# Which queue issues the first transposing loads: x tiles 1 to 3 from ScalarE, the plain loads from SyncE

## The chip, the core and the metric

The kernel runs on one core of a Trainium2 chip. The core has five engines that run side by side, each with an instruction stream of its own: TensorE (PE in the profile, with PEld for its weight loads), VectorE (DVE), ScalarE (ACT), GpSimd (POOL) and SyncE (SP). Data moves between the chip's main memory and the core's on-chip memory by DMA. In this kernel SyncE and ScalarE issue DMAs; the profile shows their issuing as SPq and ACTq, and the two queues that the issued transfers go into as q1 (SyncE's) and q10 (ScalarE's). Sixteen DMA engines serve both.

The metric is device time in microseconds (us) of one execution, median over several runs.

## The reference

One input `x` of 2048 rows by 640 columns goes through a linear-attention block (32 heads of 20) and through a gated feed-forward block (1728 wide), and a sigmoid gate per row mixes the two:

```python
def _A_ref(x, wqkv, wo):
    q, k, v = ...                                  # x @ wqkv, split by head
    phi = lambda t: jnp.where(t > 0, t + 1, jnp.exp(t)) + 1e-6
    pq, pk = phi(q), phi(k)
    kv = jnp.einsum("bhsd,bhse->bhde", pk, v)
    z = jnp.einsum("bhsd->bhd", pk)
    num = jnp.einsum("bhqd,bhde->bhqe", pq, kv)
    den = jnp.einsum("bhqd,bhd->bhq", pq, z)[..., None] + 1e-6
    ...                                            # (num / den) @ wo
def _B_ref(x, w_gate, w_up, w_down):
    return (_gelu(x @ w_gate) * (x @ w_up)) @ w_down

g = _sigmoid((x * gate_w).sum(-1, keepdims=True))
return g * _A_ref(...) + (1 - g) * _B_ref(...)
```

All inputs are bfloat16. Only `x @ wqkv` for the k and q parts, and the gate, matter for the change.

## The kernel before

The kernel is one long program without loops on the chip. A small planner (`_Plan`) takes every operation in program order with the engine it runs on, what it reads and what it writes, and puts in the semaphore waits. Each engine runs its own operations in the order in which they were written down; a DMA counts as an operation of the engine that issues it, and its completion has a semaphore of its own. So there are two kinds of order: the order on each issuing engine, fixed in the text, and the waits between engines, fixed by the data.

The stages are these. First, for each of the 16 row tiles of x (128 rows each), TensorE multiplies the transposed tile `xT` by the k weights `wk` and the q weights `wq` (640 columns each, in 5 slices of 128 rows). ScalarE takes the exponential of each product from PSUM, and VectorE makes `phi` of it. Then come the sums over all rows (`MM`), the feed-forward products (`G`, line 700, the largest part), and the output products (line 864). From tile 4 on the first stage is done by `KQ` (line 539), k and q together. The first four tiles (`NQ = 4`) are done apart: first k for tiles 0 to 3 by `KM` (lines 453 and 454), then q for them by `QM` (lines 468 and 469), so that the work can begin with only the k weights there.

The start, up to the first `QM`, is what the change touches:

- Tile 0 is loaded plainly by `load_x(0)` and transposed on TensorE by `T` (lines 433 and 437). Tiles 1 to 15 come by `load_xT` (line 353), a DMA that transposes on its way. `load_wk(k)` and `load_wq(k)` (through `dma_in`, line 341) load slice k of the weights, 160 KB in 128 rows of 1280 bytes. The gate's weights are a tiny load into `gw_sb`, after VectorE has zeroed it.
- On SyncE the order is x tile 0, wk0, xT1, wk3, wk4, xT2, xT3, wq0 to wq4, xT4 to xT15, and then the large loads. On ScalarE it is the small load `touch`, wk1, wk2, one dummy `Exp` activation, which brings in ScalarE's table, and the gate's weights.
- TensorE runs a few dummy products (`warm`), `T`, and then `KM(n, ks)` for tile n and slices ks: tile 0 with slices 0, 1, 2; tile 1 with slices 0, 1, 2; slice 3 for both tiles; `gate_col` (line 498, which turns the gate's weights into a column of `wq`); slice 4 for both tiles; then tile 2 and tile 3 whole; then `QM`.
- A product of tile n goes into the PSUM banks 2n and 2n+1 (modulo 8), and `gate_col` and `T` use banks 7 and 6 on the way. `phi1` (ScalarE, line 478) and `phi2` (VectorE, lines 488 and 492) empty the banks.

The lines that fix the order on the two issuing engines:

```python
load_x(0); load_wk(0); load_xT(1); load_wk(3); load_wk(4)   # SyncE
load_wk(1, "act"); load_wk(2, "act")                        # ScalarE, after touch
P.op("act", lambda e: e.activation(eg[:, 0:1], zero, ACT.Exp), writes=[r_eg[0]])
dma_in(gw_sb[0:5, :], ..., [r_gw], eng="act")
for i in range(2, NQ): load_xT(i)                           # SyncE again
for k in range(KC): load_wq(k)
for i in range(NQ, NT): load_xT(i)
```

Of the kernel before, what the change touches and what calls it, by code (L numbers as in the profile page):

```python
# [6 lines left out]
ACT = mybir.ActivationFunctionType  # L7
ALU = mybir.AluOpType
BF16 = mybir.dt.bfloat16
F32 = mybir.dt.float32  # L10
# [5 lines left out]
NT = S // 128  # L16
KC = D // 128
# [7 lines left out]
NQ = 4  # L25
# [137 lines left out]
def bass_gated_mix__linear_attn_block__geglu_ffn__prompt_kernel(  # L163
# [63 lines left out]
    with (  # L227
# [8 lines left out]
        with contextlib.ExitStack() as stack:  # L236
            dma_sems = [stack.enter_context(nc.semaphore("s_in%d" % i)) for i in range(n_dma_in)]

            P = _Plan(["pe", "act", "dve", "pool", "sp"])
# [9 lines left out]
            def new_dma_key():  # L249
                k = "in%d" % dma_next[0]  # L250
                dma_next[0] += 1
                return k

            def v16(o, n):
                return pool[:, o:o + n]

            def v32(o, n):
                return pool[:, o:o + 2 * n].bitcast(F32)
# [7 lines left out]
            xT = v16(R_XT, KC * S).rearrange("p (k s) -> p k s", k=KC)  # L266
# [30 lines left out]
            eg = v32(O_EG, 16)  # L297
# [3 lines left out]
            gw_sb = v16(O_GW, 128)  # L301
# [6 lines left out]
            r_xT = [P.sb("xT%d" % i, R_XT, R_XT + KC * S) for i in range(NT)]  # L308
# [25 lines left out]
            r_eg = [P.res("eg%d" % i) for i in range(NT)]  # L334
# [3 lines left out]
            r_gw = P.res("gw")  # L338

            def dma_in(dst, src, writes, reads=(), eng="sp"):  # L340
                P.op(eng, lambda e, dst=dst, src=src: e.dma_start(dst, src),  # L341
                     reads=reads, writes=writes, dma=new_dma_key())
# [3 lines left out]
            def load_x(i, eng="sp"):  # L346
                dma_in(x_aug[:, i, 0:640], A_x[0, i * 128:(i + 1) * 128, :], [r_xn[i]], eng=eng)

            def load_wk(k, eng="sp", after=()):
                dma_in(wk[:, k, :], A_wqkv[k * 128:(k + 1) * 128, 640:1280], [r_wk[k]], reads=after, eng=eng)  # L350

            def load_xT(i, after=()):
                P.op("sp", lambda e: e.dma_start_transpose(xT[:, :, i * 128:(i + 1) * 128],  # L353
                                                           A_x[0, i * 128:(i + 1) * 128, :]),
                     reads=list(after), writes=[r_xT[i]], dma=new_dma_key())

            def load_wq(k, eng="sp"):
                dma_in(wq[:, k, 0:640], A_wqkv[k * 128:(k + 1) * 128, 0:640], [r_wq[k]], eng=eng)


            P.op("act", lambda e: e.dma_start(touch[0:16, 0:4], A_wqkv[0:128:8, 640:644]),
                 writes=[P.res("touch")], dma=new_dma_key())
            load_x(0)
            load_wk(0)
            load_xT(1)
            load_wk(3)
            load_wk(4)
            load_wk(1, "act")
            load_wk(2, "act")

            zero = nc.const_aps.tensor(0.0, (128, 1), F32)
            P.op("act", lambda e: e.activation(eg[:, 0:1], zero, ACT.Exp), writes=[r_eg[0]])
            P.op("dve", lambda e: e.memset(gw_sb, 0.0), writes=[r_gw])
            dma_in(gw_sb[0:5, :], gate_w.rearrange("(k p) -> k p", p=128), [r_gw], eng="act")
            for i in range(2, NQ):
                load_xT(i)
            for k in range(KC):
                load_wq(k)
            for i in range(NQ, NT):
                load_xT(i)  # L380
            dma_in(x_aug[:, NXN:8, 0:640],
                   A_x[0, NXN * 128:8 * 128, :].rearrange("(i p) w -> p i w", p=128), r_xn[NXN:8])
# [32 lines left out]
            def warm(count, n):  # L415
                def fn(e):
                    last = None
                    for w in range(count):
                        last = e.matmul(ps[:, 4, 0:n], one_l, one_r[:, 0:n], start=True, stop=True)
                    return last  # L420
                P.op("pe", fn, writes=[bank[4]])
# [4 lines left out]
            def slot(n):  # L426
                return SLOTS[n % 4]
# [17 lines left out]
            def KM(n, ks):  # L445
                i = seq[n][1]
                b0, b1 = slot(n)

                def fn(e):
                    last = None  # L450
                    for k in ks:
                        lhs = xT[:, k, i * 128:(i + 1) * 128]
                        e.matmul(ps[:, b0, :], lhs, wk[:, k, 0:512], start=(k == 0), stop=(k == KC - 1))  # L453
                        last = e.matmul(ps[:, b1, 0:128], lhs, wk[:, k, 512:640],
                                        start=(k == 0), stop=(k == KC - 1))
                    return last
                P.op("pe", fn, reads=[r_xTa[i] if i < NXN and ks == [0] else r_xT[i]] + [r_wk[k] for k in ks],
                     writes=[bank[b0], bank[b1]])
# [37 lines left out]
            def gate_col():  # L496

                P.op("pe", lambda e: e.matmul(ps[:, 7, 0:5], gw_sb, ident[:, 0:5], start=True, stop=True),
                     reads=[r_gw, r_ident], writes=[bank[7]])
                P.op("dve", lambda e: e.tensor_copy(wq[:, :, 640:641], ps[:, 7, 0:5].unsqueeze(2)),  # L500
                     reads=[bank[7]], writes=[r_gcol])
# [4 lines left out]
            T(0, [0], 7)  # L506
            T(0, [1, 2, 3, 4], 6)
            warm(2, 128)
            for k in range(3):
                KM(0, [k])  # L510
            for k in range(3):
                KM(1, [k])
            KM(0, [3])
            KM(1, [3])
            gate_col()
            KM(0, [4])
            KM(1, [4])
            ALLK = list(range(KC))
            for n in range(2 * NQ):
                if n in (2, 3):  # L520
# [408 lines left out]
```

## Time and profile before

| what | value |
|---|---|
| time, median of 3 runs | 273.87 us (273.7 to 273.97) |
| span of the profiled execution, first to last instruction | 272.6 us |
| median of the runs less that span | 1.27 us |
| TensorE busy | 267.6 us of the span (98%) |
| mean granted TensorE clock | 1.000 |
| DVE / ACT / POOL busy | 140.8 / 75.9 / 30.0 us |
| DMA queue q1 / q10 | 23.22 MB / 0.33 MB |
| TensorE's first `KM` product, first `QM`, first `KQ` | at 4.45, 10.85 and 16.30 us |

A row of the timeline reads: start in us, duration in us, engine, line, operation, what is written and read, and in brackets how long the engine had been idle and what ended it. A row of the chain of waits reads: start, duration, engine or transfer, line. A DMA issue has two times: how long its issuing engine was busy with it, and the time from the start of issue to the landing of the last byte, the completion semaphore included. The stretches that bear on the start are the first 16 us; the table of queues can be asked for any stretch and gives the packets, the bytes and the share of the 16 DMA engines' time.

Issue and landing of each load of the start, in us (issue from the timeline, landing from the time that the list of DMA issues gives for each):

| load | queue | issue starts | landing after | lands at |
|---|---|---|---|---|
| x tile 0 | q1 | 0.79 | 2.2 | 3.0 |
| wk1 | q10 | 1.24 | 3.3 | 4.5 |
| wk0 | q1 | 1.26 | 3.1 | 4.4 |
| xT1 | q1 | 1.71 | 3.8 | 5.5 |
| wk3 | q1 | 3.06 | 3.3 | 6.4 |
| xT2 | q1 | 4.14 | 3.9 | 8.0 |
| wq0 | q1 | 6.72 | 2.7 | 9.4 |
| xT4 | q1 | 9.24 | 4.2 | 13.4 |

### The profile page before, as it was taken

The page shows a single profiled execution, that of the slowest core. Times are in us where ns is not written, and L with a number is a line of the kernel's source. Part 1 is how long each engine was busy: PE and PEld are TensorE (multiplying, and loading weights), DVE is VectorE, ACT ScalarE, POOL GpSimd, SP SyncE. Part 2 cuts the span into 40 slices and gives each one's busy share as a digit, 9 for nine tenths or more (in the row PEclk, how much of TensorE's full clock was granted, in tenths as well). Part 3 has the DMA queues.
Part 4 walks back from the last instruction along what each step waited for, and adds up shares of the span by engine and source line. Part 5 has one row for each costly group of instructions (what it writes and reads, how often), then busy time and mean ns, then how long its engine had stood idle before and what let it go on. Part 6 is the DMA issues. An engine that isn't in the chain of part 4 may idle for free.

```text
span 272.6 us, 3416 instructions
## 1 busy us (share of the span) xinstructions
PE 267.6 (98%) x1341; PEld 127.9 (47%) x1367; DVE 140.8 (52%) x247; ACT 75.9 (28%) x132; POOL 30.0 (11%) x28
## 2 busy tenths in 40 slices
PE   8999999999999999999999999999999999999997
PEld 3555555544445454444444444444444444444444
DVE  1678989997233335999999999634210000000200
ACT  2455555210422453232222233224011122121021
POOL 5000000003240002242332422000000000000000
DMA  7976999600200011514121221273031110110211
GB/s 192 202 115 127 346 399 388 140 2 19 58 19 2 23 50 51 192 34 49 26 48 25 49 48 27 60 219 105 5 77 38 41 38 19 38 41 19 58 58 41
DMA packets 42864, 23.78 MB, mean 87 GB/s; under 512 B 32223, under 2 KB 41439, under 8 KB 42719
## 3 DMA queue, kind: packets, MB, share of 16 engines
q1 hardware_dynamic: 42517, 23.22, 31.9%
q10 hardware_dynamic: 330, 0.33, 0.3%
q8 instruction: 11, 0.18, 0.3%
q14 instruction: 6, 0.05, 0.1%
HBM read 13.83 MB, written 2.63 MB: 60 GB/s over the span
## 4 chain that ended last, share of the span: by engine, by line
PE 96%; DMA 1%; SPq 1%; issue 1%; DVE 0%
PE ps L700 41%; PE ps L864 23%; PE ps L539 12%; PE ps L596 6%; PE ps L843 4%; PE ps L468 2%; PE ps L811 2%; PE ps L678 2%; PE ps L599 1%; DMA pool<-in_A_x_dram 1%; PE ps L453 1%; PE ps L824 1%; SPq L341 1%; PE ps L721 1%; SPq L353 0%
## 5 line engine op out<-in xcount | busy, mean ns | idle before, releaser
L700 PE MATMUL ps<-pool 128*128 128x512 bf16 x510 | 113.0, 379 | 0.5
L700 PEld LDWEIGHTS ps<-pool 128*128 128x128 bf16 x520 | 50.5, 98 | 60.0
L864 PE MATMUL ps<-pool 128*128 128x512 bf16 (+2 forms) x300 | 62.4, 366 | 0.3
L706 ACT ACTIVATE pool<-ps 128x512 f32<-128x512 f32 x52 | 31.0, 597 | 73.1 <-PE ps L700 73.1
L708 DVE TENSOR_TENSOR pool<-ps,pool 128x512 bf16<-128x512 f32 x52 | 34.7, 689 | 31.7 <-PE ps L700 30.4
L864 PEld LDWEIGHTS ps<-pool 128*128 128x128 bf16 x306 | 29.2, 98 | 33.4 <-issue 0.4
L847 DVE TENSOR_TENSOR pool<-ps,pool 128x512 bf16<-128x512 f32 x4 | 2.8, 690 | 61.5 <-PE ps L843 61.5
L539 PE MATMUL ps<-pool 128*128 128x512 bf16 (+1 forms) x176 | 32.5, 343 | 0.2
L754 POOL TENSOR_TENSOR pool<-pool 128x640 f32<-128x640 bf16 x16 | 22.4, 1404 | 73.0 <-DVE pool L756 65.6
L871 ACT ACTIVATE pool<-ps,pool 128x512 bf16<-128x512 f32 (+1 forms) x16 | 10.9, 680 | 68.6 <-PE ps L864 68.6
L539 PEld LDWEIGHTS ps<-pool 128*128 128x128 bf16 x180 | 17.6, 98 | 15.0
L558 DVE SCALAR_TENSOR_TENSOR pool<-ps,pool 128x128 bf16<-128x128 f32 (+2 forms) x36 | 21.7, 602 | 2.1
L549 ACT ACTIVATE pool<-ps 128x640 bf16<-128x640 f32 x24 | 16.9, 703 | 15.8 <-DVE pool L558 9.3
L596 PE MATMUL ps<-pool 128*128 128x512 bf16 x76 | 19.2, 379 | 0.1
L764 DVE TENSOR_TENSOR pool<-pool 128x640 bf16<-128x640 bf16 x16 | 13.2, 826 | 0.6
L762 DVE TENSOR_SCALAR pool<-pool 128x32 f32<-128x32 f32 x16 | 12.8, 802 | 0.6
L756 DVE TENSOR_REDUCE pool<-pool 128x32 f32<-128x640 f32 x16 | 12.9, 808 | 0.0
L644 DVE TENSOR_TENSOR pool<-pool 128x640 f32<-128x640 f32 x14 | 11.6, 826 | 0.5
L843 PE MATMUL ps<-pool 128*128 128x512 bf16 x51 | 11.5, 379 | 0.1
L646 POOL PARTITION_ALL_REDUCE pool<-pool x1 | 4.0, 3971 | 61.0 <-DVE pool L644 61.0
L596 PEld LDWEIGHTS ps<-pool 128*128 128x128 bf16 x78 | 7.0, 98 | 7.3
L555 DVE TENSOR_SCALAR pool<-pool 128x640 bf16<-128x640 bf16 x24 | 7.9, 327 | 1.7 <-ACT pool L549 0.4
(70 smaller groups left out, 124.1 us busy)
## 6 DMA issues: line engine op xcount, KB each, us to landing
out_dram<-pool SPq DMA_DIRECT2D x19, 128.0 KB, 1.7
pool<-in_B_w_gate_dram SPq DMA_DIRECT2D x1, 2080.0 KB, 14.8
pool<-in_B_w_up_dram SPq DMA_DIRECT2D x1, 2080.0 KB, 18.0
pool<-in_A_wqkv_dram SPq DMA_DIRECT2D x8, 160.0 KB, 3.1
pool<-in_A_x_dram SPq DMA_DIRECT2D x1, 1280.0 KB, 9.2
pool<-in_A_x_dram SPq DMA_DIRECT2D x1, 1120.0 KB, 6.3
pool<-in_B_w_down_dram SPq DMA_DIRECT2D x1, 1120.0 KB, 6.4
pool<-omg_row SPq DMA_DIRECT2D x1, 1024.0 KB, 4.8
```

Source lines behind the costliest of these rows:

```text
L539: last = e.matmul(ps[:, b + p, 0:c1 - c0], xT[:, k, i * 128:(i + 1) * 128], wkq[:, k, c0:c1], start=(k == 0), stop=(k == KC - 1))
L549: P.op("act", lambda e: e.activation(e_buf[m], ps_flat[:, o:o + 640], ACT.Exp), reads=banks, writes=[r_e[m]])
L558: P.op("dve", lambda e, c0=c0, c1=c1: e.scalar_tensor_tensor(dst[:, c0:c1], ps_flat[:, o + c0:o + c1], 1.0 + EPS, e_buf[m][:, c0:c1], ALU. ...
L596: last = e.matmul(ps[:, b, :], pk[i][:, c * 128:(c + 1) * 128], x_aug[:, i, 0:512], start=(i == 0), stop=(i == NT - 1))
L700: last = e.matmul(ps[:, b, :], w[:, k, fc * 128:(fc + 1) * 128], xT[:, k, j * 512:(j + 1) * 512], start=(k == 0), stop=(k == KC - 1))
L706: P.op("act", lambda e: e.activation(ge[n], ps[:, gb, :], ACT.Gelu_apprx_tanh), reads=[bank[gb]], writes=[r_ge[n]])
L708: P.op("dve", lambda e: e.tensor_tensor(hT[fc][:, j * 512:(j + 1) * 512], ps[:, ub, :], ge[n], ALU.mult), reads=[bank[ub], r_ge[n]], write ...
L754: P.op("pool", lambda e: e.tensor_tensor(tmp[n], pq[i], z_b, ALU.mult), reads=[r_pq[i], r_zb], writes=[r_tmp[n]])
L756: P.op("dve", lambda e: e.tensor_reduce(den[n], tmp[n].rearrange("p (h d) -> p h d", h=32), AX.X, ALU.add), reads=[r_tmp[n]], writes=[r_de ...
L764: P.op("dve", lambda e: e.tensor_tensor(pq[i].rearrange("p (h d) -> p h d", h=32), pq[i].rearrange("p (h d) -> p h d", h=32), den[n].unsqu ...
L843: last = e.matmul(ps[:, b, :], wd[:, fc, 512:640], hT[fc][:, j * 512:(j + 1) * 512], start=False, stop=(fc == NFC - 2), skip_group_check=True)
L864: last = e.matmul(ps[:, pb, 0:c1 - c0], lhs, rhs, start=False, stop=(q == len(rows) - 1), skip_group_check=True)
```

## The change

The three transposing loads xT1, xT2 and xT3 are issued by ScalarE, after the dummy activation and `touch`; wk1, wk2 and the gate's weights move from ScalarE to SyncE. SyncE's order becomes x tile 0, wk0 to wk4, the gate's weights, wq0 to wq4, xT4 and so on. xT4 is made to wait until xT1, xT2 and xT3 have landed. On TensorE `gate_col` moves from between slice 3 and slice 4 to behind slice 4; the rest of the order stays.

```diff
-            def load_xT(i, after=()):
-                P.op("sp", lambda e: e.dma_start_transpose(xT[:, :, i * 128:(i + 1) * 128],
+            def load_xT(i, after=(), eng="sp"):
+                P.op(eng, lambda e: e.dma_start_transpose(xT[:, :, i * 128:(i + 1) * 128],
                                                            A_x[0, i * 128:(i + 1) * 128, :]),
                      reads=list(after), writes=[r_xT[i]], dma=new_dma_key())
...
+            zero = nc.const_aps.tensor(0.0, (128, 1), F32)
+            P.op("act", lambda e: e.activation(eg[:, 0:1], zero, ACT.Exp), writes=[r_eg[0]])
             P.op("act", lambda e: e.dma_start(touch[0:16, 0:4], A_wqkv[0:128:8, 640:644]),
                  writes=[P.res("touch")], dma=new_dma_key())
             load_x(0)
-            load_wk(0)
-            load_xT(1)
-            load_wk(3)
-            load_wk(4)
-            load_wk(1, "act")
-            load_wk(2, "act")
-
-            zero = nc.const_aps.tensor(0.0, (128, 1), F32)
-            P.op("act", lambda e: e.activation(eg[:, 0:1], zero, ACT.Exp), writes=[r_eg[0]])
+            for i in range(1, NQ):
+                load_xT(i, eng="act")
+            for k in range(KC):
+                load_wk(k)
+
             P.op("dve", lambda e: e.memset(gw_sb, 0.0), writes=[r_gw])
-            dma_in(gw_sb[0:5, :], gate_w.rearrange("(k p) -> k p", p=128), [r_gw], eng="act")
-            for i in range(2, NQ):
-                load_xT(i)
+            dma_in(gw_sb[0:5, :], gate_w.rearrange("(k p) -> k p", p=128), [r_gw])
             for k in range(KC):
                 load_wq(k)
-            for i in range(NQ, NT):
+            load_xT(NQ, after=r_xT[1:NQ])
+            for i in range(NQ + 1, NT):
                 load_xT(i)
...
             warm(2, 128)
-            for k in range(3):
+            for i in range(2):
+                for k in range(3):
+                    KM(i, [k])
+            for k in (3, 4):
                 KM(0, [k])
-            for k in range(3):
                 KM(1, [k])
-            KM(0, [3])
-            KM(1, [3])
             gate_col()
-            KM(0, [4])
-            KM(1, [4])
```

## The prediction

> **What bounds the kernel now.** I read the page first, the parts for busy time and for the chain that ended last. In the chain's lines each engine or line stands with its share of the span.
>
> ```profile
> PE 267.6 (98%) x1341; PEld 127.9 (47%) x1367; DVE 140.8 (52%) x247; ACT 75.9 (28%) x132; POOL 30.0 (11%) x28
> ...
> PE 96%; DMA 1%; SPq 1%; issue 1%; DVE 0%
> ```
>
> TensorE is the bound from the first products to the end. Between 16.3 and 50 us it is busy 33.49 of 33.70 us, and VectorE, the next, 29.97. So whatever moves the first `QM` moves the end by the same amount. What is left besides TensorE lies at the start, and there the chain of waits, in order of time, was read next.
>
> ```profile
> 1.26 0.41 SPq L341
> 1.71 1.30 SPq L353
> 3.06 0.57 SPq L341
> 3.67 0.43 SPq L341
> 4.14 3.93 DMA pool<-in_A_x_dram
> 8.12 0.39 PE ps L453
> ```
>
> The chain is SyncE issuing x tile 0, wk0, xT1 (1.30 us of issue), wk3, wk4, then the landing of xT2, then tile 2's first product. Third, TensorE's timeline there:
>
> ```profile
> 4.45 0.58 PE L453 MATMUL ps<-pool 128*128 128x512 bf16 x1 [0.48 <-DMA pool<-in_A_wqkv_dram]
> ...
> 5.34 0.38 PE L453 MATMUL ps<-pool 128*128 128x512 bf16 x1
> ...
> 7.27 0.38 PE L453 MATMUL ps<-pool 128*128 128x512 bf16 x1
> ...
> 8.12 0.39 PE L453 MATMUL ps<-pool 128*128 128x512 bf16 x1 [0.42 <-DMA pool<-in_A_x_dram]
> ```
>
> A pair (512 and 128 columns) takes 0.27 us from start to start. Twenty pairs are 5.45 us; from 4.45 to 10.85 there are 6.40. The missing 0.95 is 0.35 for the first two pairs, which run slowly (0.89 instead of 0.54), 0.03 for `gate_col`, and 0.58 of waiting for xT2 (8.12 instead of 7.54). Fourth, the table of DMA queues in three stretches (packets, MB, share of 16 engines): 3.2 to 3.6, 4.4 to 4.8, and 6.4 to 7.2 us.
>
> ```profile
> q10 hardware_dynamic: 64, 0.08, 57.7%
> q1 hardware_dynamic: 61, 0.07, 46.9%
> ```
> ```profile
> q1 hardware_dynamic: 410, 0.10, 126.2%
> ```
> ```profile
> q1 hardware_dynamic: 546, 0.13, 82.4%
> ```
>
> In the first, both queues hold rows of weights and take turns, one for one. In the second there is nearly only xT1: packets of 256 bytes, so 640 for a tile's 160 KB, 0.62 us a tile at that rate. In the third xT2 and xT3: 0.94 us a tile. For plain rows, 3.6 to 4.0 had 135 packets in all, so 128 rows take 0.38 us.
>
> **The change, part by part.** Nothing is computed less, and the same bytes move. What can change is when the loads land.
>
> *Issue.* Taken off SyncE ahead of the last wq: three transposing issues, 1.30 + 2.53 = 3.83 us; put on it: wk1, wk2 (0.44 and 0.46 on ScalarE) and the gate's weights (0.57). ScalarE issues `touch` (0.42), then xT1 from about 1.3, xT2 from 2.6, xT3 from 3.9 to 5.2, against 1.71, 4.14 and 5.40 before. SyncE issues wk1 from 1.7 (was 1.24), wk2 from 2.2 (was 1.71), wk3 from 2.6 (was 3.06), wk4 from 3.1 (was 3.67), the gate from 3.5, wq0 to wq4 from 4.1 to 6.6 (was 6.72 to 9.2). What is issued behind them on ScalarE is first `phi1(0)`, at 7.47 before; its queue is free at 5.2, cover 2.2.
>
> *The table load first on ScalarE.*
>
> ```profile
> 2.20 1.28 ACT L372 ACT_TABLE_LOAD   x1 [2.20 <-issue]
> 2.27 0.57 ACTq L341 DMA_DIRECT2D pool<-in_gate_w_dram  x1
> ```
>
> The DMA written behind the activation was issued while the table was still loading. I take 0; the upper bound, if issues had to wait for the activation's end, is 1.28 + 0.20 = 1.48 us on each transposing load.
>
> *Who is served.* This decides. Before, the transposes stood in one queue with wk3 and wk4 and came in turn. Now q10 holds transposes alone and q1 an unbroken row of ten plain loads. No row shows transposes and plain rows contending in two queues for long; 4.0 to 4.4 us, the only stretch with both, has 101 packets on q10 and 126 on q1, but most of the 16 engines had but one of the two. So it is bounded from both sides. (a) Turns by packet, as at 3.2 to 3.6: a 256-byte packet waits for a 1280-byte row each time. Both queues are taken as full from 3.2 (41 packets moved from 2.8 to 3.2, 125 in the 0.4 us after), with half of wk0 still to go: q1 had moved 210 packets from 1.6 to 3.2, 128 of them x tile 0, some 18 small. A plain load then takes 0.38 + 128 of the small packets (0.62 / 640 each, 0.12) = 0.50. wk0 is through at 3.45, wk1 3.95, wk2 4.45, wk3 4.95, wk4 5.45, wq4 7.95; 0.5 more to landing, as xT1's last packets before (about 5.0) stand to its landing at 5.5. xT1 needs 640 turns, 2.5 us: through at 5.7, landed 6.2 (was 5.5). xT2: 576 of its packets by 7.95, the rest at once, landed 8.55 (was 8.04). xT3: 9.2 (was 8.8). TensorE: tile 1 begins at 6.2 and its slices 0 to 2, then slices 3 and 4 of both tiles, are seven pairs, 1.91; wk3 and wk4 have landed by then and stand queued behind tile 1. `gate_col` to 8.14; tile 2 at 8.55; ten pairs, 2.72: first `QM` at 11.27, +0.42. With 0.94 us a transpose instead of 0.62 the same steps give 0.57 a plain load, xT1 at 6.55, xT2 at 9.2, `QM` at 11.92: +1.07. (b) Turns by time, each queue half: a plain load 0.76, a transpose 1.24. wk0 lands at 4.1, wk1 4.85, wk2 5.6, xT1 4.95, wk3 6.35, wk4 7.1, xT2 6.2, xT3 7.4. Tile 0's slice 2 waits until 5.6; from there it and the seven pairs run through with `gate_col` to 7.81, and ten pairs to 10.53: -0.32. I take (a) with the faster transpose, since the only stretch with two full queues shows turns by packet, and xT1's rate was the one with its packets already queued. Rounded up towards the slower row: +0.5.
>
> [...]
>
> *xT4 waits for xT1 to xT3.* The wait on SyncE ends at xT3's landing, about 9.2, against an issue at 9.24 before; behind it stand xT5 to xT15 and all the large loads. xT4 landed 4.2 after its issue, 13.4, and `KQ(4)` began at 16.30: cover 2.9 us. Each `KQ` takes 2.7 us and each further transpose 1.36, so if xT4 isn't late none is. Cost 0; without the cover 1 us per us.
>
> *wq and the gate.* wq0 to wq4 come sooner than they did, and were needed at 10.85 and later: 0. The gate's load was issued at 2.27 and is now at 3.5, behind wk4. Were it as slow as the slowest plain load (3.3), it lands at 6.8; `gate_col` now runs after 8.1: cover 1.3. `gate_col`'s copy (0.18 on VectorE) must be through before tile 3 uses bank 7, five pairs or 1.36 us later. It costs the same 0.03 in its new place.
>
> *Sum.* Against the profiled execution's span of 272.6 us, +0.5 makes 273.1; around the span lie 1.27 us to the median of 273.87, which the change doesn't touch. The forecast is 274.4 us.
>
> **The rivals.** *Served by time*, case (b): 273.87 - 0.32 = 273.55. For it: 4.0 to 4.4 has more small packets than rows. Against it: 64 to 61 in the stretch before. *The transposes run ahead.* If q10's packets are few and start early, nothing waits: with `KM` still at 4.45, 0.58 comes back; if wk0, freed from wk1 beside it, also lands so that tile 0 starts at 4.1, 0.93. Middle 0.75: 273.1, faster. For it: xT2's issue starts 1.5 us sooner, and the wait is the chain's only transfer. Against it: wk1 and wk2 are issued 0.46 later, and five wq loads enter q1 while xT2 and xT3 are under way. This is the case on the other side; it decides once xT1 is landed by 5.4 and xT2 by 7.4. *ScalarE starts late.* The 1.48 us above: xT1 issued at 2.8, lands at 6.6 with its old 3.8; xT2 under case (a) at about 9.6; ten pairs from there give 12.3, +1.45: 275.3. The gate's issue at 2.27 speaks against it. *The change doesn't do what it says* has a form too: if both issuing engines share what makes the packets, the transposes' 1.3 us of issue also hold up the plain loads, the order is as serial as before, and the time lies near 273.9; wk1, on an empty q10, had only 5 packets on that queue before 3.2 though issued at 1.24. It falls between the first two cases and has its chance in (b).
>
> **How the numbers follow.** Forecast, case (a): 0.45; its own range is +0.3 to +1.1, 274.2 to 275.0. Served by time, with the serial form: 0.25. Transposes ahead: 0.18. ScalarE late: 0.12. A difference within 0.2% (0.55 us, so 273.32 to 274.42) is about what a measurement can't tell from no change. Case (a) puts 0.27 above that and 0.18 within; by time 0.21 within, 0.04 faster; ahead 0.16 faster, 0.02 within; late 0.12 slower. Sums: faster 0.20, same 0.41, slower 0.39. The forecast lies at the edge between the two. The range leaves out the best of the cases ahead and the far end of the late one: 273.2 to 275.2.
>
> **What would show it.** In the changed kernel's TensorE timeline, a wait for `in_A_x_dram` ahead of tile 1 (near 5.4 to 6.2) that wasn't there, and tile 2's first product at about 8.5; wk3 landed long before its product. Case (b) shows instead short waits for `in_A_wqkv_dram` in tile 0. The case ahead shows tile 2 right behind `gate_col`, before 7.8. The late case shows the first transposing ACTq issue at 2 us or later. If xT4's landing came after 16, or `phi1(0)` waited for ScalarE's issuing, the parts costed at nothing would be wrong.

## The result, and the profile after

| | before | after |
|---|---|---|
| median | 273.98 us (273.7 to 275.07, 6 runs) | 276.99 us (275.78 to 278.47, 6 runs) |
| ratio, 95% interval | | 1.0108 (1.0085 to 1.013) |
| span of the profiled execution | 272.6 us | 275.6 us |
| first `KM`, first `QM`, first `KQ` | 4.45, 10.85, 16.30 | 4.29, 13.78, 19.23 |

The change costs 3.0 us, about 1.1%; the forecast was 274.4 us, with a range to 275.2. All of it is in the first stretch: from the first `QM` to the end of the span it is 261.78 us before and 261.79 after. The first `QM` is 2.93 us later. The page of the changed kernel, busy time and chain:

```profile
PE 269.7 (98%) x1341; PEld 128.4 (47%) x1367; DVE 140.7 (51%) x247; ACT 76.0 (28%) x132; POOL 30.0 (11%) x28
...
PE 96%; DMA 2%; issue 1%; SPq 0%; DVE 0%
```

TensorE's busy time has grown by 2.1 us with the same 1341 instructions: something runs slower, not only later. The chain of waits at the start:

```profile
1.26 0.41 SPq L341
1.72 0.43 SPq L341
2.19 5.06 DMA pool<-in_A_wqkv_dram
7.29 0.61 PE ps L450
...
8.00 0.43 PE ps L450
...
8.54 0.43 PE ps L450
```

Before, it ran through xT2. Now it runs through wk2, a plain load of 160 KB that takes 5.06 us from its issue at 2.19 to its landing at 7.25, and then through products that follow each other at twice the old distance. TensorE's timeline shows both (lines 450 and 451 are the old 453 and 454):

```profile
4.29 0.59 PE L450 MATMUL ps<-pool 128*128 128x512 bf16 x1
4.67 0.31 PE L451 MATMUL ps<-pool 128*128 128x128 bf16 x1
6.46 0.58 PE L450 MATMUL ps<-pool 128*128 128x512 bf16 x1 [1.48 <-DMA pool<-in_A_wqkv_dram]
...
7.80 0.63 PE L450 MATMUL ps<-pool 128*128 128x512 bf16 x1
...
8.33 0.63 PE L450 MATMUL ps<-pool 128*128 128x512 bf16 x1
...
10.46 0.41 PE L450 MATMUL ps<-pool 128*128 128x512 bf16 x1
...
10.76 0.38 PE L450 MATMUL ps<-pool 128*128 128x512 bf16 x1
```

A wait for wk1 of 1.48 us, and pairs at 0.53 us until 10.46, where they fall to 0.27. Before, that step came at 5.3. The table of queues for 3.2 to 8.2 us (packets, MB, share of the 16 DMA engines), first the kernel before, then the changed one:

```profile
q1 hardware_dynamic: 2416, 0.95, 89.0%
q10 hardware_dynamic: 293, 0.32, 18.2%
```
```profile
q1 hardware_dynamic: 484, 0.56, 71.5%
q10 hardware_dynamic: 1287, 0.32, 44.3%
```

The shares sum to more than 1 in both (107% and 116%): the DMA engines are not short of work. Yet they deliver 0.88 MB instead of 1.27 in these 5 us.

### The profile page after: what moved, and what is told of

Its sections match the earlier page's. It is cut to its first block, busy times and chain, and to the rows that moved or that the text cites. A ratio compares the mean times of both kernels' runs of the same rounds, so it can differ in the third digit from the quotient of the medians.

```text
span 275.6 us, 3417 instructions
## 1 busy us (share of the span) xinstructions
PE 269.7 (98%) x1341; PEld 128.4 (47%) x1367; DVE 140.7 (51%) x247; ACT 76.0 (28%) x132; POOL 30.0 (11%) x28
## 4 chain that ended last, share of the span: by engine, by line
PE 96%; DMA 2%; issue 1%; SPq 0%; DVE 0%
PE ps L695 41%; PE ps L859 23%; PE ps L534 12%; PE ps L591 6%; PE ps L838 4%; PE ps L450 2%; DMA pool<-in_A_wqkv_dram 2%; PE ps L806 2%; PE ps L465 2%; PE ps L673 2%; PE ps L594 1%; PE ps L819 1%; PE ps L451 1%; PE ps L716 1%; SPq L341 0%
## 5 line engine op out<-in xcount | busy, mean ns | idle before, releaser
L695 PE MATMUL ps<-pool 128*128 128x512 bf16 x510 | 113.0, 379 | 0.5
L591 PE MATMUL ps<-pool 128*128 128x512 bf16 x76 | 19.2, 379 | 0.1
L751 DVE TENSOR_REDUCE pool<-pool 128x32 f32<-128x640 f32 x16 | 12.9, 809 | 0.0
L838 PE MATMUL ps<-pool 128*128 128x512 bf16 x51 | 11.5, 379 | 0.1
L450 PE MATMUL ps<-pool 128*128 128x512 bf16 x19 | 7.6, 481 | 1.6 <-DMA pool<-in_A_wqkv_dram 1.5
```

Of the source, the lines that this page charges most:

```text
L591: last = e.matmul(ps[:, b, :], pk[i][:, c * 128:(c + 1) * 128], x_aug[:, i, 0:512], start=(i == 0), stop=(i == NT - 1))
L695: last = e.matmul(ps[:, b, :], w[:, k, fc * 128:(fc + 1) * 128], xT[:, k, j * 512:(j + 1) * 512], start=(k == 0), stop=(k == KC - 1))
L838: last = e.matmul(ps[:, b, :], wd[:, fc, 512:640], hT[fc][:, j * 512:(j + 1) * 512], start=False, stop=(fc == NFC - 2), skip_group_check=True)
```

## The experiments

Theory A: transposing packets in one queue and plain rows in the other hinder each other on the DMA engines, so that the loads land late. Its rivals are named in the expectations. Each expectation was written before its run. Landings are those of each run's profiled execution, issue plus time to landing.

**Plain loads in place of the transposing ones**, in the same 256-byte pieces:

```diff
-                load_xT(i, eng="act")
+                dma_in(xT[:, :, i * 128:(i + 1) * 128],
+                       A_x[0, i * 128:(i + 1) * 128, :].rearrange("p (k s) -> p k s", k=KC), [r_xT[i]], eng="act")
```

> The changed kernel, with x tiles 1 to 3 loaded plainly by ScalarE into the same place, in the same 640 pieces of 256 bytes a tile: the transposition of these three tiles is left out, queues and order stay. Theory A (transposing packets in one queue and plain rows in the other hinder each other on the DMA engines): wk1 lands by about 5.0 us instead of 6.3, wk3 by 7 instead of 9.2, no wait over 0.5 us inside tiles 0 and 1, time 273.0 to 274.0. Rival B (turns by packet between two full queues, whatever is in them): the landings stay within 0.5 us of the changed kernel's and the time is 276 or more.

Measured: 276.22 us, ratio 1.0079 (1.0063 to 1.0095); wk1 at 5.82, wk3 at 7.91, a wait of 1.17 us for wk1. Neither theory's numbers. The queues for 3.2 to 8.2 us:

```profile
q1 hardware_dynamic: 819, 0.93, 54.9%
q10 hardware_dynamic: 1926, 0.48, 42.8%
```

1.41 MB, with as many packets a tile as the transposing loads have (640). So pieces of 256 bytes don't bring what the engines deliver down to 0.88 MB; transposing does. By these rows (share times 16 engines times 5 us, over the packets) a packet on q1 takes 54 ns on average; by the rows of the changed kernel above it takes 118. But 1926 of the small pieces moved on q10 to 819 packets on q1, and wk1 still lands 1.2 us after TensorE wanted it (4.6), and the time is hardly better than after. That was the first sign that the loads are not all of it: pairs stayed at 0.53 us until 9.99.

**The queues swapped**, transposing loads on SyncE, wk0 to wk4 on ScalarE:

```diff
             for i in range(1, NQ):
-                load_xT(i, eng="act")
+                load_xT(i)
             for k in range(KC):
-                load_wk(k)
+                load_wk(k, "act")
```

> The changed kernel with the two queues swapped: SyncE issues xT1 to xT3 behind x tile 0, ScalarE issues wk0 to wk4; the rest of SyncE's order stays. Theory A: the same hindrance, wk3 lands after 8 us, time 275.5 to 277.5. Rival D (a transposing load issued by ScalarE is what is slow): wk3 lands by 6.5, time at most 274.3.

Measured: 277.94 us, 1.0139 (1.0113 to 1.0166), 0.4 above A's range; wk3 at 9.63. With the transposing loads on SyncE the plain rows land as late (wk3 at 9.23 in the changed kernel). D falls.

**Dummy products in the wait for wk1:**

```diff
                     KM(i, [k])
+                    if (i, k) == (0, 0):
+                        warm(3, 512)
```

> The changed kernel with three more dummy products of 512 columns behind the first pair of tile 0, where TensorE waits for wk1 anyway. If the slow pairs (0.53 us each instead of 0.27, eight of them) are the loss (rival C), the first QM comes 2.1 us sooner and the time is 274.9. Under theory A the pairs run at 0.27, but slice 3 can't begin before wk3 lands at 9.2; from there 14 pairs and gate_col are 3.8 us, the first QM is at 13.1 instead of 13.8, time 276.3.

Measured: 276.09 us, 1.0079 (1.0055 to 1.0103), 0.9 below the changed kernel; the first `QM` at 13.05, wk3 at 8.94, wk4 at 9.64. As A has it: from wk4's landing twelve pairs and `gate_col` are 3.3 us, which makes 12.9. With the pairs at 0.27 from 8.26 on, what remains is the late landing.

**wq0 to wq4 held back** until xT1 and xT2 have landed (`load_wq` hands `after` on as reads):

```diff
-                load_wq(k)
+                load_wq(k, after=r_xT[1:3])
```

> The changed kernel with wq0 held on SyncE, and all behind it, until xT1 and xT2 have landed, so that only wk0 to wk4 and the gate's weights stand in q1 beside the transposing loads. Rival B in the form of the prediction (the unbroken row of ten plain loads takes the turns): wk3 lands by 7 us and the time falls below 275. Theory A: wk1 to wk3 land within 0.7 us of the changed kernel's, only xT2 and xT3 come sooner; time 276.0 to 277.5.

Measured: 277.67 us, 1.0128 (1.0102 to 1.0154); wk1 at 7.12, wk3 at 9.81, xT2 at 9.77. Without a single wq in the queue the wk loads land no sooner. The prediction's mechanism, ten plain loads that outlast the transposing ones, falls. A's numbers are missed by a little: wk1 is 0.79 us later than in the changed kernel instead of within 0.7, xT2 doesn't come sooner (9.29 there), and the time is 0.2 above the range.

**One queue for all** (the small load and the zeroing of the gate's buffer are tied to each other, to order the small load's end):

```diff
             load_x(0)
-            for i in range(1, NQ):
-                load_xT(i, eng="act")
-            for k in range(KC):
+            load_wk(0)
+            load_xT(1)
+            for k in range(1, KC):
                 load_wk(k)
...
+            for i in range(2, NQ):
+                load_xT(i)
```

> The changed kernel with every load of the start on SyncE, in one queue: x tile 0, wk0, xT1, wk1 to wk4, xT2, xT3, the gate's weights, wq0 and so on; ScalarE keeps only the small touch load. Theory A (the loss is made where two queues alternate on the DMA engines): the packets flow as in the kernel before, and only issue time counts: wk3 is issued near 4.0 and lands by 7.3, xT2 near 8.8, time 274.3 to 275.0. Rival E (too many loads in flight from the start, whatever the queue): wk3 lands after 8.5, time 276 or more.

Measured: wk3 issued at 4.15 and landed at 7.25, xT2 at 8.77, as A has it; 3.1 and 3.7 us to landing against 6.6 and 6.7 after. The time, 275.98 us (1.0062, 1.0042 to 1.0082), is a miss: the gate's load now stood behind xT3 and landed at 9.79, and TensorE waited for it 0.83 us ahead of tile 2. The expectation forgot that load. TensorE also waited 1.71 us for wk1, which was issued only at 3.06, behind xT1.

**The small parts alone**, on the kernel before (the first added line stands ahead of `touch`):

```diff
+            P.op("act", lambda e: e.activation(eg[:, 0:1], zero, ACT.Exp), writes=[r_eg[0]])
...
+            load_xT(NQ, after=r_xT[1:NQ])
...
-            gate_col()
             KM(0, [4])
             KM(1, [4])
+            gate_col()
```

> The kernel before with the three small parts of the change and none of the moved loads: the dummy activation first on ScalarE, gate_col behind slice 4, xT4 waiting for xT1 to xT3. Both theories price them at nothing: 273.7 to 274.2, within 0.2% of the kernel before. If one of them counts, it is 274.5 or more.

Measured: 274.0 us, 0.9991 (0.9974 to 1.0007). They cost nothing.

**Equal rows in both queues:**

```diff
-                load_xT(i, eng="act")
+                dma_in(x_aug[:, i, 0:640], A_x[0, i * 128:(i + 1) * 128, :], [r_xn[i], r_xq[i]], eng="act")
...
```

> The changed kernel with x tiles 1 to 3 loaded by ScalarE as plain rows of 1280 bytes, untransposed, and the transposing loads of these tiles on SyncE after that; the products of tiles 1 to 3 in this stage take tile 0 as their left side, so their k and q are left out. Two queues, but equal rows in both and nothing transposed until they have landed. If small pieces are what hinders (theory A refined: small packets and rows alternating), the flow is that of the first microseconds of the kernel before: wk1 lands by 5.0, wk3 by 6.5, wk4 by 7.0, time 273.0 to 274.0. If any second queue hinders, wk3 lands after 7.5 and the time is 275.5 or more.

The loads did what the first branch says, near enough: wk1 at 5.53, wk2 at 6.16, wk3 at 6.93, wk4 at 7.35, and 1.81 MB in 3.2 to 8.2 us. The time did what the second says: 276.05 us, 1.0073 (1.0048 to 1.0097). Its TensorE timeline has the reason:

```profile
5.66 0.58 PE L453 MATMUL ps<-pool 128*128 128x512 bf16 x1 [0.56 <-DMA pool<-in_A_wqkv_dram]
...
6.71 0.63 PE L453 MATMUL ps<-pool 128*128 128x512 bf16 x1
...
8.84 0.63 PE L453 MATMUL ps<-pool 128*128 128x512 bf16 x1
...
9.38 0.40 PE L453 MATMUL ps<-pool 128*128 128x512 bf16 x1
9.61 0.22 PE L454 MATMUL ps<-pool 128*128 128x128 bf16 x1
```

After a wait of 0.56 us and from 6.21 on none, pairs run at 0.53 until 9.38. Eighteen pairs at 0.27 and `gate_col` would have brought the first `QM` at 11.1; it came at 12.68. So 1.5 us are lost with no load late. New theory, C2, the author's conjecture from this run: TensorE runs its pairs at 0.27 only after some microseconds of nearly unbroken work (here 3.7, from the end of the wait at 5.66 to the first fast pair at 9.38), and a pause in that time starts the count anew.

**Tile 1 transposed on TensorE**, an attempt at a faster kernel:

```diff
-NXN = 1
+NXN = 2
...
-            load_xT(1)
+            load_x(1)
...
+            T(1, [0], 7)
+            T(1, [1, 2, 3, 4], 6)
```

> The kernel before with tile 1 treated as tile 0 is: loaded plainly by SyncE and transposed on TensorE, so one transposing load less stands ahead of wk3, wk4 and xT2. xT2 is issued 0.85 us sooner and the wait of 0.58 before tile 2 goes; five more small products cost 0.3. Expected 273.5 to 273.9; it is slower than the kernel before if VectorE's two copies hold up tile 1 by more than 0.3.

Measured: 274.25 us, 1.0006 (0.999 to 1.0022), the same. xT2 landed at 7.53 instead of 8.07, and TensorE waited instead 0.29 us for x tile 1 and then for wk2, which landed at 6.21 (4.88 before).

**The rows again, with the pause filled:**

```diff
                     KM(i, [k])
+                    if (i, k) == (0, 0):
+                        warm(1, 512)
+                        warm(2, 128)
```

> The kernel with plain rows for x tiles 1 to 3 (their k and q left out as there), with one dummy product of 512 and two of 128 columns behind the first pair of tile 0, which fill the 0.7 us in which TensorE waited for wk1. The loads landed in time there (wk2 at 6.2, wk4 at 7.4), yet eight pairs ran at 0.53 us. If that slow running is set by TensorE's own pause (theory C2), the pairs from 6.2 on run at 0.27, the first QM comes at 11.1 to 11.4 instead of 12.7, time 274.2 to 274.8. If the slow running has to do with the loads' traffic, the pairs stay at 0.53 and the time at 276.

Measured: 275.23 us, 1.0049 (1.0024 to 1.0073), between the two. The six runs lie apart: 274.51, 274.61, 274.68, and 275.78, 276.12, 276.61. The lower three are what C2 promised, the upper three what the traffic would give; the profiled execution is the one of 276.12. In it wk0 landed at 4.77, TensorE paused 0.73 us ahead of tile 0, worked without a pause from 4.91, and still ran at 0.53 until 9.77. So this run decides nothing between the two; what sets the two groups apart isn't settled.

**The first dummy products taken away**, loads as before:

```diff
-            warm(5, 512)
-            warm(1, 128)
```

> The kernel before, loads untouched, without the six dummy products that run ahead of tile 0's transposition. Theory C2: TensorE begins its busy time 2.2 us later, so it reaches full speed about 2.2 us later, at 7.3 instead of 5.1; five to eight more pairs at 0.53, 1.3 to 2.1 us, of which the wait of 0.58 for xT2 takes up a part: time 274.6 to 275.5. If the slow pairs come from the loads, it is 274.0.

Measured: 274.69 us, 1.0021 (1.0001 to 1.0041). The loads landed as before (xT2 at 8.02), and the pairs were slow until 7.64:

```profile
4.98 0.63 PE L453 MATMUL ps<-pool 128*128 128x512 bf16 x1
...
7.11 0.63 PE L453 MATMUL ps<-pool 128*128 128x512 bf16 x1
...
7.64 0.38 PE L453 MATMUL ps<-pool 128*128 128x512 bf16 x1
```

Six slow pairs instead of two, with no change to any load: the four more don't come from the loads, and what TensorE did before counts, as the first half of C2 has it. TensorE was ready for tile 2 at 8.75 instead of 7.54, 1.21 later, of which the old wait of 0.58 for xT2 takes up its part; the first `QM` came at 11.47, +0.62.

**The wait for wk0 filled**, on the kernel before:

```diff
-            warm(2, 128)
+            warm(6, 128)
```

> The kernel before with six instead of two dummy products of 128 columns between tile 0's transposition and its first pair, which fill the 0.48 us of waiting for wk0. C2: the two slow pairs may become one or none, but the wait for xT2 takes up what is gained, since the chain runs through that load: 273.7 to 274.2, the same, with less scatter. It is slower by up to 0.2 if the dummies outlast the wait.

Measured: 273.94 us, 0.9995 (0.9985 to 1.0005). No gain: in the profiled execution no pair is slow, but xT2 landed at 8.39 and TensorE waited 0.64 us for it ahead of tile 2. No version tried beats the kernel before.

**xT1 held until wk0 to wk2 have landed:**

```diff
-                load_xT(i, eng="act")
+                load_xT(i, eng="act", after=r_wk[0:3])
```

(The loop now stands behind that of the wk loads.)

> The changed kernel with xT1 held on ScalarE until wk0, wk1 and wk2 have landed, so that nothing transposing is in flight beside these three. Theory A: wk0 to wk2 land 0.4 to 0.5 us apart, wk1 by 4.9 and wk2 by 5.4 (6.3 and 7.3 in the changed kernel); xT1 then lands near 9, TensorE has paused and runs slowly, and the time is 276.5 to 278.5. If the late landing of wk1 and wk2 is due to the order on SyncE alone, they land after 6.

Measured: wk0 at 3.57, wk1 at 5.00, wk2 at 5.45, so the late landing isn't the order on SyncE. The time is 281.58 us (1.0278, 1.0254 to 1.0302), a miss by 3 us, and it shows the hindrance from the other side. Issued at 5.55, xT1 met the five wq loads; the list of DMA issues for the moment of its issue (columns: what, queue, count, size, us to landing):

```profile
pool<-in_A_x_dram ACTq DMA_TRANSPOSE x1, 6.1
```

It landed at 11.64, right after the last wq at 11.42; xT2 and xT3 followed at 12.17 and 12.67. Beside each other both were slow: xT1 took 6.1 us to landing (3.8 in the kernel before), wq0 and wq1 3.9, wq2 to wq4 4.6 to 5.6 (2.7 to 3.3 before).

Two runs speak against the second half of C2, that a pause starts the count anew. The kernel before paused 0.48 us right ahead of its first pair, at 4.45, and ran at 0.27 a pair two pairs later, from 5.34 on. And in the run with wq0 to wq4 held back the slow pairs came behind fast ones. The table of stretches there (stretch, length, busy time of the engines from PE to POOL, granted clock, share and GB/s of the DMA engines):

```profile
4.60:7.90 3.30, 0.99 (x5) 0.37 (x6) 0.00 (x0) 0.00 (x0) 0.10 (x1) 1.00 1.20 170
8.00:11.30 3.30, 3.30 (x13) 1.29 (x12) 0.00 (x0) 0.00 (x0) 0.00 (x0) 0.50 0.82 136
11.40:14.00 2.60, 2.60 (x21) 1.51 (x21) 1.77 (x5) 2.00 (x3) 0.00 (x0) 1.00 0.92 276
```

Its first pairs, at 4.69 and 7.25, are fast in spite of a wait of 2.13 us for wk1 between them; then the granted clock is 0.50 from 8.0 to 11.3 us, while TensorE works without a stop (3.30 us busy of 3.30). A wait of 1.71 us in the run with one queue was followed by fast pairs alone, from 6.30 on. So what TensorE did before counts, as the run without dummy products shows, but not by the length of a pause alone; the rule is not shown.

## Why the prediction was wrong

Step by step, as the prediction put them:

- *TensorE bounds the rest, a later first `QM` moves the end one for one.* Right to 0.01 us.
- *Issue.* Right: xT1 at 1.28, xT2 at 2.58, xT3 at 3.92; wk1 at 1.72, wk2 at 2.19. wk4 was 0.25 and the gate's load 0.5 later than put. The table load costs nothing: ScalarE issued `touch` and xT1 beside it (0.85 and 1.28, table load 0.78 to 2.06). The late case is out.
- *Who is served.* This step failed, in both of its terms. The packets of the two queues did not come one for one: from 3.2 to 8.2 us q10 moved 1287 while q1 moved 484, 2.7 to one. (That most of the 16 engines had but one of the two queues' packets from 4.0 to 4.4 us in the kernel before was the author's reading; no view shows the engines singly.) And a packet doesn't keep its old time: a packet on q1 took 118 ns on average, against 49 by the prediction's own row for q1 from 3.2 to 3.6 us, and a transposing packet 28, against 20 by its row for 4.4 to 4.8. So a weight load does not come 0.38 + 0.12 = 0.50 us behind the one ahead of it: wk1 to wk4 landed 1.09 us apart on average. With equal rows in both queues it was 0.61, with plain pieces of 256 bytes 0.87: of what lies above 0.61, the small pieces make about half and the transposing the rest. The table sets forecast and landing side by side; the plain rows, which were to win the turns, are the latest. Of the signs that the prediction named, that of case (b) came, a wait for weights in tile 0, but of 1.48 us.

| lands at, us | wk1 | wk2 | wk3 | wk4 | xT1 | xT2 | xT3 |
|---|---|---|---|---|---|---|---|
| before | 4.50 | 4.88 | 6.37 | 6.83 | 5.53 | 8.07 | 8.77 |
| forecast, case (a) | 4.45 | 4.95 | 5.45 | 5.95 | 6.2 | 8.55 | 9.2 |
| after | 6.33 | 7.25 | 9.23 | 9.60 | 7.46 | 9.29 | 11.37 |
| plain pieces of 256 bytes in place of transposing | 5.82 | 6.79 | 7.91 | 8.43 | - | - | - |
| equal rows in two queues | 5.53 | 6.16 | 6.93 | 7.35 | - | - | - |
| nothing transposing beside wk0 to wk2 | 5.00 | 5.45 | 5.90 | 6.76 | - | - | - |

  With fast products, slice 3 would start at wk3's landing, 9.23, and slice 4 right behind it; fourteen pairs and `gate_col`, 3.85 us, would put the first `QM` at 13.1. So about 2.2 of the 2.93 us are the late landing, which the run with dummy products (13.05) bears out.
- *The first two pairs run slowly, 0.35 us.* Taken over as a constant, it was the second failure: eight pairs were slow instead of two. Net of the waits for wk3 and wk4 it is the other 0.7 us (13.78 less 13.1; the dummy products brought the first `QM` 0.73 sooner). The number isn't fixed even with the same order of loads: the run with the small parts alone has no slow pair in its profiled execution, the run without dummy products six. How many of the eight the wait for wk1 made isn't shown.
- *xT4's wait at nothing.* Right: xT4 was issued at 11.46, landed 2.8 later at 14.23, and `KQ(4)` began at 19.23.
- *wq and the gate at nothing.* They cost nothing, the gate by luck. The wq loads came later than before, not sooner (11.13 to 12.82 against 9.40 to 12.05); for a first `QM` at the forecast's 11.27, wq0 would have been 0.14 ahead. The gate's load landed at 10.29 instead of by 6.8; had `gate_col` come after 8.14 as forecast, TensorE would have waited some 2.1 us for it. It came at 11.04.
- *The rivals.* None had the case that came. All four priced the two queues with the service times of a queue alone.

What stays open: why transposing packets and plain rows slow each other. That they do when they come from two queues, whichever issues which, is shown (wk3 at 9.23 and 9.63, against 6.93 with equal rows); no view shows what happens inside a DMA engine. Open too is what decides when TensorE's pairs go from 0.53 to 0.27 us.

## What to carry to other kernels

Before moving transposing loads to a queue of their own, ask what plain loads will be in flight beside them: here the two together moved 0.88 MB where equal rows moved 1.81 in the same 5 us. At a kernel's start, price a wait of TensorE by two terms, the wait itself and the products that may run at 0.53 us a pair instead of 0.27 after it, and take the second as a range: with the same order of loads it was none or two pairs here. A rate that a row shows for a queue alone was not the rate of two queues here: a transposing packet took 20 ns nearly alone and 28 beside plain rows.

## What the runs showed of the hardware that was not expected

- A load of weights of 160 KB took 2.7 to 3.3 us from issue to landing in the kernel before, 3.0 to 4.4 with equal rows in both queues, and 4.6 to 6.6 (wk1 to wk4) beside transposing loads in the other queue.
- The sixteen DMA engines showed a share of 116% in the changed kernel and delivered a third less than at 107% before: 0.88 MB against 1.27 from 3.2 to 8.2 us.
- In the changed kernel's profile the granted clock is 1.00 in every stretch of the start, while pairs take 0.53 us instead of 0.27: there only the distance between products tells of it. In the run with wq0 to wq4 held back, where fast pairs came first, the row did tell: 0.50 from 8.0 to 11.3 us.
